# Moving columns of rounded fp32 matmuls read in pairs from both halves, PSUM written in the same order

## The chip, the cores and the metric

The kernel runs on one core of one Trainium2 chip. The metric is the device time of one execution in microseconds; the median of several runs is compared. A core has five engines that run their own queues and wait for each other by semaphores: PE (matrix products; the profile shows its weight loads apart, as PEld), DVE (vector work), ACT (functions and copies), POOL (general vector work, and a DMA queue) and SP (issues most DMAs). Matmuls write PSUM, eight banks of 512 fp32 columns on each of 128 partitions; only DVE and ACT read it here. Everything else works on SBUF.

## The reference

A layer norm feeds two branches, full attention with 32 heads of 18 features over 2048 tokens, and a gated feed-forward block of 4608 hidden features. Their product is added to the input:

```python
def reference(A_x, A_wqkv, A_wo, B_x, B_W_gate, B_W_up, B_W_down):
    # S = 2048 tokens, D = 576, H = 32 heads, F = 4608
    ...
        p = _softmax(scores, axis=-1)
        o = jnp.einsum("bhqk,bhkd->bhqd", p, v)
    ...
        gate = gate * (lambda x, dt: x.astype(dt))(gate > 0, gate.dtype)
        h = gate * up
        return jnp.einsum("bsf,fd->bsd", h, W_down)

    xn = _layernorm(x, axis=-1)
    s = _A_ref(xn, A_wqkv, A_wo)
    g = _silu(_B_ref(xn, B_W_gate, B_W_up, B_W_down))
    return x + s * g
```

All inputs and the output are fp32.

## The kernel before

**Products in three parts.** Most fp32 operands are split into two rounded numbers of the type float32r: `hi`, the value rounded, and `lo`, what is left. A product is then three matmuls of rounded operands (`PRODUCTS`: hi by hi, hi by lo, lo by hi), all added up in one PSUM bank. Only the product of the softmax terms with the values (tile `po`) is of plain fp32.

**A matmul's two operands.** `nc.tensor.matmul(ps, l, r)` loads `l`, the stationary operand (up to 128 columns), into the array and streams `r`, the moving operand, through it, column by column: 512 columns in most products here, 288 (half of D) in the others. For each moving column one column of `ps` is written or added to. All matmuls of the kernel go through the helper `mm` (line 274), so they all have the profile's line L275; the tiles tell them apart.

**Two lanes.** A matmul over 64 rows uses half of the array's rows. The kernel keeps two such streams going, lane 0 on partitions 0 to 63 and lane 1 on 64 to 127, each writing a bank of its own at any time. The class `Lanes` writes out PE's order by hand: it keeps a clock for each lane, charges a matmul `cols * COL + FIX` us (COL 0.000446, FIX 0.006), and picks the next matmul, the bank and the engine that empties it from these estimates. A sum of many matmuls (`Part`) begins in one lane and is ended in the other. `keep` holds the instructions in the order in which they are recorded.

**The stages.** First the tokens are normalized and transposed (`tps`), in four groups of 512. Their products with the attention weights give queries and keys (`pq`, 512 columns) and values (`pv`, 288 columns). From then on the feed-forward block and the attention share PE, in cycles: `pg` and `pu` are the gate and up products (512 columns), `py` the down product (288 columns), `pm` and `psx` are the two passes over the attention scores (512 columns; the first for the row maxima, the second for the exponentials), `po` the product with the values. DVE reduces `pm` to maxima (L401), ACT turns `psx` into exponentials (L891), DVE and ACT empty the others, and POOL splits the weights (L312, L313) and the hidden features (L744, L747). At the end the attention's output weights are applied (`pw`, 288 columns, all 128 rows at once, one matmul after the other).

**The warm-up.** `busy` (line 607) keeps PE at work while the first loads arrive: 8 matmuls on a tile of ones, then 24 on `xr`, a rounded copy of the first tokens. Its results are not used. The 24 differ, four by four, in the order in which the moving columns are read (`mixed`), and the last four have 32 stationary columns in place of 128. PSUM is written in order in all of them.

Of the kernel before, what the change touches and what calls it, by code (L numbers as in the profile page):

```python
# [10 lines left out]
F32R = mybir.dt.float32r  # L11
# [206 lines left out]
def kernel(  # L218
# [10 lines left out]
    nc = tc.nc  # L229
    P = 128  # L230
# [34 lines left out]
    def keep(ins):  # L265
        return tc.keep_in_program_order(ins)
# [4 lines left out]
        ins = nc.sync.dma_start(*args)  # L271
        return keep(ins) if in_order[0] else ins

    def mm(*args, **kw):
        return keep(nc.tensor.matmul(*args, **kw))  # L275

    def tp(*args):
        return keep(nc.tensor.transpose(*args))
# [14 lines left out]
    def bank(b, name):  # L293
        return banks.tile([P, 512], F32, tag=f"b{b}", name=name)

    def fence(by, ps):
        eng = {"A": nc.scalar, "V": nc.vector}[by]
        eng.clobber_nop(outs=[eng.lower_ap(ps)])

    lanes = Lanes(8, bank, mm, fence)  # L300

    def lane_rows(lane):
# [128 lines left out]
    with ExitStack() as st:  # L431
# [175 lines left out]
        def busy(xt):  # L607

            ones = one.tile([P, 512], F32R, name="ones")
            xr = one.tile([P, 576], F32R, name="xr")  # L610
            root = one.tile([P, 1], F32, name="root")
            nc.gpsimd.memset(ones.bitcast(F32), 1.0)
            nc.scalar.activation(root, ident[:, :1], AF.Sqrt)
            nc.scalar.activation(xr, xt[:, 0], AF.Copy)
            ps = bank(7, "wu")
            def mixed(form, **n):
                return xr[:, :512].rearrange(f"p {form}", **n)

            ops = [(ones[:, :P], ones)] * 8 + [(xr[:, :P], xr[:, :512])] * 4
            ops += [(xr[:, :P], mixed("(a b) -> p b a", b=2))] * 4  # L620
            ops += [(xr[:, :P], mixed("(a b) -> p b a", a=2))] * 4
            ops += [(xr[:, :P], mixed("(a b) -> p b a", b=16))] * 4
            ops += [(xr[:, :P], mixed("(a b c) -> p b a c", a=32, c=4))] * 4
            ops += [(xr[:, :32], xr[:, :512])] * 4
            for l, r in ops:
                m = l.shape[1]
                to = ps[:m]
                if len(r.shape) == 3:
                    to = to.rearrange("p (a b) -> p a b", b=r.shape[2])
                if len(r.shape) == 4:  # L630
                    to = to.rearrange("p (a b c) -> p a b c", b=r.shape[2], c=r.shape[3])
                mm(to, l, r, start=True, stop=True)
            nc.scalar.activation(root, ps[:, :1], AF.Copy)

        ln0 = []
        xt0 = load_rows(0)
        busy(xt0)
        for _ in stats(xt0, ln0):
            pass
# [267 lines left out]
    def attend(u, qp):  # L907

        va = vas[u % 2]
        b, ps = lanes.hold("po")  # L910
        batch = sorted(ready, key=lambda r: r[0])
        for n, (kt, p) in enumerate(batch):
            for i in range(2):
                for h in range(2):
                    s_ = 32 * (2 * h + i)
                    mm(
                        ps[s_ : s_ + 32, :], va[:, kt, h * VA : h * VA + 32], p[:, h, i, :],
                        start=(n == 0), stop=(n == len(batch) - 1), skip_group_check=True,
                    )
        end = lanes.pause(len(batch) * 0.86 + 0.3)  # L920
        ready.clear()

        def copy(ps):
            ots.append(two.tile([P, 512], F32, name="ot", bufs=2))
            nc.scalar.activation(ots[0], ps, AF.Copy)

        def add(ps):
            ot = ots.pop()
            keep(nc.vector.tensor_tensor(ot, ps, ot, ALU.add))  # L929
            later.append(divide(u, qp, ot))  # L930

        lanes.evict(b, ps, end, [("V", 0.69, add)] if ots else [("A", 0.6, copy)])
# [35 lines left out]
    for k in range(0, N1, 2):  # L968
# [6 lines left out]
        n = 7 if i % 2 == 0 else 6  # L975
# [83 lines left out]
    def any_bank(name):  # L1059
        turns[0] += 1  # L1060
        return bank(turns[0] % 8, name)
# [27 lines left out]
    for j in range(4):  # L1089
        js = slice(j * P, (j + 1) * P)  # L1090
        for n in range(2):
            cs = halves[n]
            ps = any_bank("py")[:, :HC]
# [8 lines left out]
    for i, k in enumerate(horder):  # L1102
# [8 lines left out]
        for cs in halves:  # L1111
            ps = any_bank("pw")[:, :HC]
# [39 lines left out]
```

## Time and profile before

| what | value |
|---|---|
| median of 3 runs | 2610.64 us (2610.39 to 2611.22) |
| the profiled execution | 2609.53 us, its span 2607.8 us |
| PE busy | 2575.4 us, 25308 matmuls |
| DVE, ACT, POOL busy | 1785.9, 1471.0, 1440.5 us |
| moved by DMA | 241.85 MB, mean 93 GB/s |

The span is the time from the first to the last instruction that the profiler saw. A matmul's row gives its start and its duration; durations of matmuls that follow each other overlap, because they are pipelined, so the pace is read from one start to the next. In a name such as `64*128 64x512` the first part is the stationary operand (rows by columns), the second the moving one.

### The profile page before, as it was taken

What the parts mean: (1) busy time and instruction counts of PE and PEld (TensorE: products, weight loads), DVE (VectorE), ACT (ScalarE), POOL (GpSimd) and SP (SyncE); (2) the same over time, 40 slices, a digit from 0 to 9 for tenths busy, and PEclk for the clock granted to TensorE, in tenths of its full rate; (3) what the DMA queues carried; (4) which work ended last, traced back from release to release, by engine and by line L of the source; (5) the groups of instructions that cost most, each with busy time, mean ns of one, the idle gap of its engine ahead of it and who ended that gap; (6) DMA issues with size and microseconds to landing.
All of it is one profiled execution on the core that took longest, in us unless ns stands there. A gap on an engine that the chain in (4) does not pass through costs nothing.

```text
span 2607.8 us, 62736 instructions
## 1 busy us (share of the span) xinstructions
PE 2575.4 (99%) x25308; PEld 2106.7 (81%) x25308; DVE 1785.9 (68%) x2976; ACT 1471.0 (56%) x2763; POOL 1440.5 (55%) x1276
## 2 busy tenths in 40 slices
PE   8999999999999999999999999999999999999998
PEld 6998887777778887777778778788878777777778
DVE  4326557777777777777777777777777777776137
ACT  3221136666666666666666666666666666666662
POOL 4236885555555555555555555555555555555554
PEclk8999999999999999999999999999999999999999
DMA  7645332222332222222242222222232222222237
GB/s 240 219 150 150 88 103 69 78 70 72 98 100 66 76 69 75 69 70 75 74 133 72 71 72 67 74 66 77 72 114 82 66 77 72 74 67 58 58 113 214
DMA packets 270353, 241.85 MB, mean 93 GB/s; under 512 B 33904, under 2 KB 214896, under 8 KB 270064
## 3 DMA queue, kind: packets, MB, share of 16 engines
q1 hardware_dynamic: 262000, 209.53, 27.5%
q0 software_dynamic: 8064, 28.32, 3.3%
q8 instruction: 200, 3.28, 0.5%
q14 instruction: 89, 0.73, 0.1%
HBM read 192.79 MB, written 44.96 MB: 91 GB/s over the span
## 4 chain that ended last, share of the span: by engine, by line
PE 92%; DMA 3%; POOL 2%; DVE 1%; SPq 1%; issue 1%; ACT 0%; POOLq 0%; DVEq 0%; ACTq 0%
PE pg L275 19%; PE po L275 17%; PE py L275 16%; PE pu L275 15%; PE pm L275 10%; PE psx L275 9%; PE pq L275 3%; PE pv L275 2%; SPq L271 1%; PE pw L275 1%; DMA rgw<-in_A_wqkv_dram 0%; DMA qd<-hh 0%; DMA gt<-yd 0%; DMA rg<-in_B_W_up_dram 0%; DMA kT<-kd 0%
## 5 line engine op out<-in xcount | busy, mean ns | idle before, releaser
L401 DVE TENSOR_REDUCE mx<-pm 128x1 f32<-128x512 f32 x2048 | 1378.5, 689 | 351.5 <-PE pm L275 207.1
L891 ACT ACTIVATE p<-psx 128x512 f32<-128x512 f32 x2048 | 1181.9, 598 | 567.4 <-PE pm L275 279.3
L275 PE MATMUL pg<-x,gw 64*128 64x512 f32 x3888 | 1155.2, 391 | 1.8 <-POOL gw L313 1.8
L275 PE MATMUL pu<-x,gw 64*128 64x512 f32 x3888 | 1141.7, 391 | 0.0
L275 PE MATMUL pm<-kT,qT 54*128 54x512 f32 x2048 | 792.2, 397 | 0.7 <-DMA kT<-kd 0.7
L275 PE MATMUL psx<-qT,kT 56*128 56x512 f32 x2048 | 786.7, 394 | 0.0
L275 PEld LDWEIGHTS pg<-x,gw 64*128 64x128 f32 x3888 | 718.5, 186 | 43.4 <-POOL gw L313 2.7
L275 PEld LDWEIGHTS pu<-x,gw 64*128 64x128 f32 x3888 | 716.2, 186 | 33.5
L275 PE MATMUL py<-dw,hh 64*128 64x288 f32 x6864 | 720.3, 295 | 5.7 <-DVE ot L929 3.1
L275 PEld LDWEIGHTS py<-dw,hh 64*128 64x128 f32 x6864 | 665.4, 186 | 74.2 <-issue 53.4
L275 PE MATMUL po<-p,va 128*32 128x512 f32 x4096 | 452.7, 594 | 0.4 <-ACT p L891 0.4
L744 POOL CAST hh<-h 128x512 fp32r<-128x512 f32 x127 | 77.6, 611 | 607.2 <-DVE h L741 607.2
L313 POOL TENSOR_TENSOR gw<-rg,gw 128x1152 fp32r<-128x1152 f32 x144 | 383.7, 2665 | 11.6
L275 PEld LDWEIGHTS psx<-qT,kT 56*128 56x128 f32 x2048 | 375.3, 185 | 17.8
L275 PEld LDWEIGHTS pm<-kT,qT 54*128 54x128 f32 x2048 | 371.6, 185 | 15.6 <-DVE mx L401 0.9
L771 POOL TENSOR_TENSOR y<-yt,y 128x288 f32<-128x288 f32 x268 | 215.0, 806 | 297.8 <-ACT yt L770 297.6
L275 PEld LDWEIGHTS po<-p,va 128*32 128x32 f32 x4096 | 126.4, 110 | 279.1 <-issue 269.1
L313 POOL TENSOR_TENSOR dw<-rd,dw 128x576 fp32r<-128x576 f32 x144 | 212.2, 1474 | 11.5
L747 POOL TENSOR_TENSOR hh<-h,hh 128x512 fp32r<-128x512 f32 x144 | 186.2, 1293 | 33.2 <-ACT hh L746 23.1
L312 POOL CAST gw<-rg 128x1152 fp32r<-128x1152 f32 x144 | 165.0, 1146 | 23.4 <-DMA rg<-in_B_W_up_dram 9.5
L766 DVE TENSOR_TENSOR y<-py,y 128x288 f32<-128x288 f32 x268 | 120.0, 448 | 58.7 <-PE py L275 58.5
L929 DVE TENSOR_TENSOR ot<-po,ot 128x512 f32<-128x512 f32 x32 | 22.1, 691 | 188.4 <-PE po L275 188.4
(92 smaller groups left out, 1421.2 us busy)
## 6 DMA issues: line engine op xcount, KB each, us to landing
rd<-in_B_W_down_dram SPq DMA_DIRECT2D x144, 288.0 KB
rg<-in_B_W_gate_dram SPq DMA_DIRECT2D x144, 256.0 KB
rg<-in_B_W_up_dram SPq DMA_DIRECT2D x144, 256.0 KB
qT<-qd SPq DMA_DIRECT2D x384, 36.0 KB
kT<-kd SPq DMA_DIRECT2D x384, 36.0 KB
kd<-hh POOLq DMA_DIRECT2D x16, 512.0 KB, 5.5
qd<-hh POOLq DMA_DIRECT2D x16, 512.0 KB, 6.1
xTd<-x SPq DMA_DIRECT2D x15, 512.0 KB
```

What stands on the lines that cost most here:

```text
L271: ins = nc.sync.dma_start(*args)
L275: return keep(nc.tensor.matmul(*args, **kw))
L312: keep(nc.gpsimd.tensor_copy(hi, raw))
L313: keep(nc.gpsimd.tensor_tensor(lo, raw, hi.bitcast(F32), ALU.subtract))
L401: keep(nc.vector.tensor_reduce(mx[:, g % 2, h, j, c : c + 1], ps, axis=AX.X, op=ALU.max))
L744: keep(nc.gpsimd.tensor_copy(hh[:, 0], h))
L747: keep(nc.gpsimd.tensor_tensor(hh[:, 1], h, hh[:, 0].bitcast(F32), ALU.subtract))
L766: keep(nc.vector.tensor_tensor(ys[j][:, cs], ps[:, :HC], ys[j][:, cs], ALU.add))
L771: keep(nc.gpsimd.tensor_tensor(ys[j][:, cs], t, ys[j][:, cs], ALU.add))
L891: nc.scalar.activation(p[0][:, h, i, :], ps, AF.Exp, scale=SCALE)
L929: keep(nc.vector.tensor_tensor(ot, ps, ot, ALU.add))
```

## The change

`mm` now looks at the moving operand. If that is float32r and a plain two-dimensional view, both it and the PSUM view are given another order of columns by `paired`: with n columns, the order is 0, 1, n/2, n/2+1, 2, 3, n/2+2, n/2+3 and so on. Each moving column still ends in the PSUM column of its own number, so nothing else has to know of it. The stationary operand, the plain fp32 products (`po`) and the transposes (`tp`) stay as they are. The planner's constants in `Lanes` stay too.

The warm-up gets another list: 18 matmuls on ones in order, then three each of six orders, with `ones` as the stationary operand. In five of them PSUM is written in the order of the reading, in the last one in sequence (`both` is 0). Views with more than two dimensions pass through `mm` unchanged. `mm` moves from line 275 to line 281.

```diff
-    def mm(*args, **kw):
-        return keep(nc.tensor.matmul(*args, **kw))
+    def paired(t):
+        return t.rearrange("p (a b c) -> p b a c", a=2, c=2)
+
+    def mm(ps, l, r, **kw):
+
+        if r.dtype == F32R and len(r.shape) == 2:
+            ps, r = paired(ps), paired(r)
+        return keep(nc.tensor.matmul(ps, l, r, **kw))
...
             ps = bank(7, "wu")
-            def mixed(form, **n):
-                return xr[:, :512].rearrange(f"p {form}", **n)
-
-            ops = [(ones[:, :P], ones)] * 8 + [(xr[:, :P], xr[:, :512])] * 4
-            ops += [(xr[:, :P], mixed("(a b) -> p b a", b=2))] * 4
-            ops += [(xr[:, :P], mixed("(a b) -> p b a", a=2))] * 4
-            ops += [(xr[:, :P], mixed("(a b) -> p b a", b=16))] * 4
-            ops += [(xr[:, :P], mixed("(a b c) -> p b a c", a=32, c=4))] * 4
-            ops += [(xr[:, :32], xr[:, :512])] * 4
-            for l, r in ops:
...
+            ops = [(ones, 512, 1, 512, 1)] * 18
+            ops += [(xr, 512, 2, 2, 1)] * 3 + [(xr, 512, 2, 4, 1)] * 3 + [(xr, 512, 4, 2, 1)] * 3
+            ops += [(xr, 512, 2, 8, 1)] * 3 + [(xr, 288, 2, 2, 1)] * 3 + [(xr, 288, 2, 1, 0)] * 3
+            for r, n, a, c, both in ops:
+                r, to = (t[:, :n].rearrange("p (a b c) -> p b a c", a=a, c=c) for t in (r, ps))
+                if not both:
+                    to = ps[:, :n].rearrange("p (b a c) -> p b a c", a=a, c=c)
+                mm(to, ones[:, :P], r, start=True, stop=True)
```

More of the change, by code (lines that the diff above doesn't have):

```diff
@@ L615, in busy @@
             ps = bank(7, "wu")
-            def mixed(form, **n):
-                return xr[:, :512].rearrange(f"p {form}", **n)
-            ops = [(ones[:, :P], ones)] * 8 + [(xr[:, :P], xr[:, :512])] * 4
-            ops += [(xr[:, :P], mixed("(a b) -> p b a", b=2))] * 4
-            ops += [(xr[:, :P], mixed("(a b) -> p b a", a=2))] * 4
-            ops += [(xr[:, :P], mixed("(a b) -> p b a", b=16))] * 4
-            ops += [(xr[:, :P], mixed("(a b c) -> p b a c", a=32, c=4))] * 4
-            ops += [(xr[:, :32], xr[:, :512])] * 4
-            for l, r in ops:
[L626 to L632, printed above, removed]
+            ops = [(ones, 512, 1, 512, 1)] * 18
[6 more added lines that the diff above has]
+                mm(to, ones[:, :P], r, start=True, stop=True)
             nc.scalar.activation(root, ps[:, :1], AF.Copy)
```

## The prediction

> **What bounds the kernel now.** I read the page's shares first, then the chain of waits, then PE's groups by form, then single matmuls on the timeline.
>
> ```profile
> span 2607.8 us, 62736 instructions
> PE 2575.4 (99%) x25308; PEld 2106.7 (81%) x25308; DVE 1785.9 (68%) x2976; ACT 1471.0 (56%) x2763; POOL 1440.5 (55%) x1276
> PE 92%; DMA 3%; POOL 2%; DVE 1%; SPq 1%; issue 1%; ACT 0%; POOLq 0%; DVEq 0%; ACTq 0%
> ```
>
> PE is never idle for more than 32.4 us in all, and 92% of the chain that ended last is PE behind itself. So the end is set by how fast matmuls follow each other, and that is what the change touches. Busy share alone does not tell the pace, since matmuls overlap. The pace comes from start times; the counts come from the groups (line, engine, tiles, stationary and moving shape, count | busy us, mean ns | idle before):
>
> ```profile
> L275 PE MATMUL pg<-x,gw 64*128 64x512 f32 x3888 | 1155.2, 391 | 1.8 <-POOL gw L313 1.8
> L275 PE MATMUL pu<-x,gw 64*128 64x512 f32 x3888 | 1141.7, 391 | 0.0
> L275 PE MATMUL pm<-kT,qT 54*128 54x512 f32 x2048 | 792.2, 397 | 0.7 <-DMA kT<-kd 0.7
> L275 PE MATMUL psx<-qT,kT 56*128 56x512 f32 x2048 | 786.7, 394 | 0.0
> L275 PE MATMUL py<-dw,hh 64*128 64x288 f32 x6816 | 712.2, 295 | 2.7 <-POOL dw L313 1.5 <-ACTq L298 0.2
> L275 PE MATMUL po<-p,va 128*32 128x512 f32 x4096 | 452.7, 594 | 0.4 <-ACT p L891 0.4
> L275 PE MATMUL pq<-x,wqk 64*128 64x512 f32 x972 | 124.0, 398 | 0.7 <-ACT x L519 0.7
> L275 PE MATMUL pv<-wv,x 64*128 64x288 f32 x864 | 65.4, 299 | 9.0 <-DVEq L298 9.0
> L275 PE MATMUL pw<-wo,hf 128*128 128x288 f32 x384 | 56.3, 295 | 0.5 <-DVE hf L1067 0.5
> ```
>
> All but po have rounded fp32 on the moving side, so all but po are changed. Two-lane matmuls of 512 columns: 3888 + 3888 + 2048 + 2048 + 972 = 12844, two at a time, so 6422 slots. Two-lane matmuls of 288: 6816 + 864 = 7680, so 3840 slots. About 496 of 288 columns use all 128 rows and run alone (384 here, 64 more of pw, 48 of py at the end).
>
> The slots, on the timeline (start us, us, engine, line):
>
> ```profile
> 1500.71 0.39 PE L275 MATMUL pu<-x,gw 64*128 64x512 f32 x1
> 1500.94 0.39 PE L275 MATMUL pu<-x,gw 64*128 64x512 f32 x1
> ...
> 1503.04 0.40 PE L275 MATMUL pu<-x,gw 64*128 64x512 f32 x1
> 1503.21 0.29 PE L275 MATMUL py<-dw,hh 64*128 64x288 f32 x1
> ...
> 1503.34 0.29 PE L275 MATMUL py<-dw,hh 64*128 64x288 f32 x1
> 1503.47 0.39 PE L275 MATMUL pm<-kT,qT 54*128 54x512 f32 x1
> 2575.71 1.76 PE L275 MATMUL pw<-wo,hf 128*128 128x288 f32 x12
> ```
>
> In one lane a 512-column matmul starts every (1503.04 - 1500.71) / 10 = 0.233 us. A 288-column one lasts to the next start 0.13 us. The lone pw run gives the third digit: (1.76 - 0.29) / 11 = 0.134 us. So a slot costs 0.0025 to 0.006 us plus about 0.445 ns a column. The sum of slots: 6422 x 0.2335 = 1500, 3840 x 0.134 = 515, 496 x 0.134 = 66, and po 453: 2534 us of the 2607.8. The rest is idle time, warm-up, transposes and lanes alone.
>
> **What reading order does to the pace.** The warm-up in busy() already holds matmuls of 512 columns that differ only in the order of their moving columns. By the code's order they are, four each: contiguous; every second column; a column of the first half and one of the second by turns; every sixteenth column; runs of four, 64 bytes apart; contiguous with 32 stationary columns.
>
> ```profile
> PEclk8999999999999999999999999999999999999999
> 5.04 1.91 PE L275 MATMUL wu<-xr 128*128 128x512 f32 x4
> 7.20 1.53 PE L275 MATMUL wu<-xr 128*128 128x512 f32 x3
> 8.11 0.63 PE L275 MATMUL wu<-xr 128*128 128x512 f32 x1
> 8.79 0.81 PE L275 MATMUL wu<-xr 128*128 128x512 f32 x3
> 9.22 0.38 PE L275 MATMUL wu<-xr 128*128 128x512 f32 x1
> 9.86 1.48 PE L275 MATMUL wu<-xr 128*128 128x512 f32 x3
> 10.72 0.61 PE L275 MATMUL wu<-xr 128*128 128x512 f32 x1
> 11.40 0.83 PE L275 MATMUL wu<-xr 128*128 128x512 f32 x3
> 11.84 0.39 PE L275 MATMUL wu<-xr 128*128 128x512 f32 x1
> 12.30 0.85 PE L275 MATMUL wu<-xr 128*32 128x512 f32 x3
> 12.77 0.39 PE L275 MATMUL wu<-xr 128*32 128x512 f32 x1
> ```
>
> Each row of three with the row of its last gives two steps: every second column (8.11 - 7.20) / 2 = 0.455; halves by turns 0.215; every sixteenth 0.43; runs of four 0.22; contiguous with 32 columns 0.235. The first row, (1.91 - 0.63) / 3 = 0.427, is contiguous at what I take for a reduced clock: the page's clock row is below 9 in its first slice, and the later contiguous rows are near 0.233. So at the clock of the main loops contiguous reading costs 0.233, here and in the loops, while halves by turns cost 0.215, 8% less. Order of reading alone moves the pace, both ways.
>
> The new order is 0, 1, 256, 257, 2, 3, ...: by turns between the halves like the 0.215 row, with two neighbours each time like a contiguous read. I expect no less than the 0.215 row's pace from the read. The Trainium skill, Advanced Engine Details and Errata, section SBUF Cachelines, says that two accesses to the same 16-byte line are needed for full pace. This trace disagrees: halves by turns never hit a line twice in a row and are the fastest row; by that rule the new order would be as good as the old, and the sum would be nothing.
>
> **The change part by part.** *Instructions.* The order of all engines stays; only PE's warm-up is another list, and a few waits of PE on PE are new. PE's start, before (wu is the warm-up's bank, ones and xr its operands):
>
> ```order
> L275 MATMUL wu<-ones 128x512 x8
> L275 MATMUL wu<-xr 128x512 x20
> L275 MATMUL wu<-xr 32x512 x4
> L278 MATMUL tps<-ident,xn 128x64 x24
> L275 MATMUL pq<-x,wqk_167 128x512 x13
> ```
>
> and now:
>
> ```order
> L281 MATMUL wu<-ones 128x512 x18
> L281 MATMUL wu<-xr,ones 128x128x2x2 x3
> L281 MATMUL wu<-xr,ones 128x64x2x4 x3
> L281 MATMUL wu<-xr,ones 128x64x4x2 x3
> L281 MATMUL wu<-xr,ones 128x32x2x8 x3
> L281 MATMUL wu<-xr,ones 128x72x2x2 x3
> L281 MATMUL wu<-xr,ones 128x288 x3
> L284 MATMUL tps<-ident,xn 128x64 x24
> L281 MATMUL pq<-x,wqk_171 128x128x2x2 x13
> ```
>
> The transposes and pq stand where they stood. Warm-up, 32 before, 36 now: some 14 at 0.427, 4 at 0.233, 12 at 0.215 and 6 at 0.124 make 10.2 us against 11.6; at 0.43 for the odd ones 13 or 14. I count 0, with 2 us either way.
>
> *New waits.* PE rows that wait on PE's own semaphore rise from 15 to 156. A typical place is after a batch of po (p are softmax terms, va values), before:
>
> ```order
> L275 MATMUL po<-p,va_3011 32x512 [waits Activation_49]
> L275 MATMUL po<-p,va_3011 32x512
> L275 MATMUL py<-dw,hh 128x288 [waits DVE_49,Pool_49]
> L275 MATMUL py<-dw,hh 128x288 x3
> L275 MATMUL py<-dw,hh 128x288 [waits Pool_49]
> ```
>
> and now:
>
> ```order
> L281 MATMUL po<-p,va_3015 32x512 [waits Activation_49]
> L281 MATMUL po<-p,va_3015 32x512
> L281 MATMUL py<-dw,hh 128x72x2x2 [waits DVE_49,Pool_49]
> L281 MATMUL py<-dw,hh 128x72x2x2 [waits PE_49]
> L281 MATMUL py<-dw,hh 128x72x2x2 x2
> L281 MATMUL py<-dw,hh 128x72x2x2 [waits Pool_49]
> ```
>
> The second py, the other lane's first, now waits for a matmul that stands ahead of the whole po batch, done microseconds earlier. All of PE queues behind it, but there is nothing left to wait for: 0, at most 141 x 0.134 = 19 us if each lost a slot.
>
> *The read.* 512 columns: lower bound 0.215, upper bound inside a gain 0.2225 (runs of four). I take 0.217, next to the row it resembles most. Gain 6422 x (0.2335 - 0.217) = 106 us. 288 columns have no row; scaled, 0.121 (0.215 x 288 / 512) to 0.128. I take 0.1245: 3840 x 0.0095 = 36 us, and 496 x 0.0095 = 5 us. Sum 147 us. po keeps its 453.
>
> *The write.* No matmul of this trace writes PSUM out of order. The nearest rows are the reads: between 0.215 (halves by turns) and 0.455 (every second column) for 512. I take no cost, because pairs stay neighbours and the warm-up's jumps over half a tile were free on the read side. The other end is a rival below. The Trainium skill speaks on both sides: PSUM — Partial Sum Buffer, section Specifications (TRN2), says that any non-contiguous pattern slows matmuls significantly, and Advanced Engine Details and Errata, section PSUM Cachelines, asks only that every two consecutive elements be contiguous, which this order keeps. No run here shows either.
>
> *What could take the gain back.* Issue and weight loads must follow a 0.062 us step in py:
>
> ```profile
> 13.09 0.97 PE L278 MATMUL tps<-ident,xn 64*128 64x64 f32 x24
> L275 PEld LDWEIGHTS py<-dw,hh 64*128 64x128 f32 x6816 | 657.5, 186 | 70.2 <-issue 49.5 <-POOL dw L313 3.3 <-ACTq L298 2.4
> L275 PEld LDWEIGHTS po<-p,va 128*32 128x32 f32 x4096 | 126.4, 110 | 279.1 <-issue 269.1 <-ACT p L891 10.0
> 0.00:60.00 60.00, 48.90 (x388) 38.18 (x388) 29.40 (x69) 19.72 (x42) 30.17 (x28) 0.93 0.73 226
> 270.00:330.00 60.00, 57.44 (x594) 50.92 (x592) 31.80 (x56) 10.07 (x22) 50.46 (x48) 1.00 0.33 97
> 500.00:1000.00 500.00, 500.00 (x4917) 396.65 (x4915) 376.46 (x615) 312.25 (x580) 273.82 (x239) 1.00 0.27 80
> ```
>
> 24 transposes with their loads went out in 0.97 us, 0.040 each, so issue is not the limit. A load of 128 columns lasts 186 ns, of 32 columns 110: 0.79 ns a column, estimated 0.101 us of a lane's 0.1245. That is close, and cuts py's gain if I am 0.02 off. In the windows (length, then busy us of PE, PEld, DVE, ACT, POOL; granted clock; DMA share and GB/s) DVE fills 75% of the steady stretch and would fill 80%, ACT and POOL less. At 270 to 330 us POOL is at 84% with PE at 96%, and in the first 60 us PE is busy for 48.9 only, with the transfers at 0.73; there some of the gain is lost. I take off 12 us, 6% of 200 us of such stretches.
>
> Net 147 - 12 = 135. The profiled execution took 2609.53 us (span 2607.8, 1.7 around it): 2474.5, and the median of the runs is 1.1 above it: **2475 us**. Its own range: all at 0.215 and 0.121, nothing lost, gain 6422 x 0.0185 + 4336 x 0.013 = 175, so 2435; at 0.2225 and 0.128 with 20 lost, 71 + 26 - 20 = 77, so 2530.
>
> **The rivals.** *The write sets the pace.* If each step to another place in PSUM costs as a read of every sixteenth or second column does, a 512 slot takes 0.43 to 0.455 and a 288 slot 0.242 to 0.256. Added: 6422 x 0.1965 + 4336 x 0.108 = 1730 us to 6422 x 0.2215 + 4336 x 0.122 = 1951: about 4340 to 4560 us. It decides as soon as a paired slot costs over 0.2335. For it: an access of another place each time doubled two warm-up rows. Against: two others lost nothing. The rule of the Trainium skill's page PSUM — Partial Sum Buffer, named above, would end here.
>
> *Only 288 columns are slow.* Their halves lie 576 bytes apart, not 1024, and no row shows that distance. At 0.256 they cost 4336 x 0.122 = 529 us more and 512 gains its 106: about 3030. Smaller mixtures of either kind end between 2616 and 3000.
>
> *Nothing changes.* If 0.233 is the price of two lanes' loads and not of the order, the time stays at 2610. Against it: the lone-lane contiguous rows have the same 0.235 and 0.134. Half of the gain (288 unmoved, new waits at their bound) would be 2520 to 2600.
>
> **How the numbers follow.** Both sides follow the fast row 0.55, a smaller gain 0.07, within 0.2% (what a measurement of this kernel can tell from no change) 0.06, slower up to 3030 us 0.13, the write at about double 0.19. Faster 0.62, same 0.06, slower 0.32. The range runs from 2435 to 3050: 0.81 less a little at its low end. Forecast alone: 2435 to 2530.
>
> **What would show it.** Right: in the new trace pg and pu of one lane start 0.215 to 0.22 us apart, py 0.122 to 0.127; po stays at 453 us busy; the warm-up rows of shape 128x2x2 step by 0.215 and DVE's share rises to 72%. Wrong on the write: the 128x2x2 warm-up rows, which read and write in that order, step above 0.233. Wrong on 288: py alone above 0.134. If pg steps at 0.217 and the time hardly falls, waits on DVE, POOL or loads stand in PE's idle time.

## The result, and the profile after

The changed kernel takes 3425.22 us (median of 4 runs, 3424.29 to 3427.13) against 2610.93 us for the kernel before (4 runs): 1.312 times as long, with an interval of 1.3097 to 1.3143. The forecast was 2475 us, so even the direction was wrong, and the time lies beyond the upper end of the range, 3050 us. No rival had this time either: it lies between the 3030 us of slow 288-column products and the 4340 us of a slow write.

The page of the changed kernel begins so (span; busy us and share by engine; the chain that ended last, by engine):

```profile
span 3425.4 us, 62804 instructions
PE 3410.8 (100%) x25312; PEld 2665.8 (78%) x25312; DVE 1831.4 (53%) x2976; ACT 1522.0 (44%) x2763; POOL 1428.6 (42%) x1276
PE 97%; DMA 1%; issue 1%; SPq 1%; POOL 1%; DVE 0%; POOLq 0%; ACT 0%; DVEq 0%; ACTq 0%
```

Idle time of PE falls from 32.4 to 14.6 us (3425.4 - 3410.8). No new wait holds PE up; it is PE itself that takes longer. The groups by form (busy us, mean ns of one) say which matmuls:

```profile
L281 PE MATMUL pg<-x,gw 64*128 64x512 f32 x3888 | 1554.2, 503 | 0.0
L281 PE MATMUL pu<-x,gw 64*128 64x512 f32 x3888 | 1541.3, 501 | 0.0
L281 PE MATMUL pm<-kT,qT 54*128 54x512 f32 x2048 | 1011.1, 504 | 0.0
L281 PE MATMUL psx<-qT,kT 56*128 56x512 f32 x2048 | 1001.5, 503 | 0.0
L281 PE MATMUL py<-dw,hh 64*128 64x288 f32 x6816 | 954.4, 361 | 0.0
L281 PE MATMUL po<-p,va 128*32 128x512 f32 x4096 | 452.7, 594 | 0.0
```

Every kind whose columns were reordered grew: pg from 391 to 503 ns, py from 295 to 361. po, which keeps its order, has the same 452.7 us to the tenth. The timeline gives the step from start to start in one lane, and the last row a run of lone matmuls of 288 columns:

```profile
1500.33 0.51 PE L281 MATMUL pg<-x,gw 64*128 64x512 f32 x1
...
1500.66 0.50 PE L281 MATMUL pg<-x,gw 64*128 64x512 f32 x1
...
1503.30 0.50 PE L281 MATMUL pg<-x,gw 64*128 64x512 f32 x1
...
3369.68 2.04 PE L281 MATMUL pw<-wo,hf 128*128 128x288 f32 x10
```

From 1500.33 to 1503.30 that lane has nine steps, 0.330 us each, where it was 0.233. The pw run steps by (2.04 - 0.36) / 9 = 0.187 us, where it was 0.134. With the prediction's counts, 6422 x (0.330 - 0.2335) + 4336 x (0.187 - 0.134) = 620 + 230 = 850 us. The time grew by 814. Of the 36 us between, 18 are PE's idle time that fell; where the other 18 went was not traced. So the whole loss stands in the slots, and the question is which side of the reordering makes them longer. The changed kernel's own warm-up can't tell: its three matmuls that read and write in the new order start 0.33 us apart (the first at 7.35, the third at 8.01 us). That is the sign by which the prediction would have called the write wrong, but these matmuls reorder both sides, as the loops do.

### The profile page after: what moved, and what is told of

Same layout as the page of the kernel before. It is cut to its first block, busy times and chain, and to the rows that moved or that the text cites. A ratio compares the mean times of both kernels' runs of the same rounds, so it can differ in the third digit from the quotient of the medians.

```text
span 3425.4 us, 62804 instructions
## 1 busy us (share of the span) xinstructions
PE 3410.8 (100%) x25312; PEld 2665.8 (78%) x25312; DVE 1831.4 (53%) x2976; ACT 1522.0 (44%) x2763; POOL 1428.6 (42%) x1276
## 4 chain that ended last, share of the span: by engine, by line
PE 97%; DMA 1%; issue 1%; SPq 1%; POOL 1%; DVE 0%; POOLq 0%; ACT 0%; DVEq 0%; ACTq 0%
PE pg L281 24%; PE py L281 18%; PE pu L281 14%; PE po L281 13%; PE psx L281 11%; PE pm L281 10%; PE pq L281 4%; PE pv L281 2%; PE pw L281 1%; DMA rgw<-in_A_wqkv_dram 1%; SPq L271 0%; DMA qd<-hh 0%; POOL wqk L319 0%; DMA o<-od 0%; PE tps L284 0%
## 5 line engine op out<-in xcount | busy, mean ns | idle before, releaser
L888 ACT ACTIVATE p<-psx 128x512 f32<-128x512 f32 x2048 | 1208.9, 598 | 1117.6 <-PE psx L281 746.1
L281 PE MATMUL pg<-x,gw 64*128 64x512 f32 x3888 | 1554.2, 503 | 0.0
L281 PE MATMUL pu<-x,gw 64*128 64x512 f32 x3888 | 1541.3, 501 | 0.0
L281 PE MATMUL pm<-kT,qT 54*128 54x512 f32 x2048 | 1011.1, 504 | 0.0
L281 PE MATMUL psx<-qT,kT 56*128 56x512 f32 x2048 | 1001.5, 503 | 0.0
L281 PE MATMUL py<-dw,hh 64*128 64x288 f32 x6864 | 964.4, 361 | 3.6 <-DVE ot L926 3.6
L281 PEld LDWEIGHTS py<-dw,hh 64*128 64x128 f32 x6864 | 861.0, 193 | 101.8 <-issue 55.6
L281 PEld LDWEIGHTS pg<-x,gw 64*128 64x128 f32 x3888 | 754.0, 194 | 160.2
L281 PEld LDWEIGHTS pu<-x,gw 64*128 64x128 f32 x3888 | 753.2, 194 | 66.5
L281 PE MATMUL po<-p,va 128*32 128x512 f32 x4096 | 452.7, 594 | 0.0
L281 PE MATMUL pq<-x,wqk 64*128 64x512 f32 x972 | 171.0, 501 | 0.3 <-ACT x L525 0.2
```

Of the source, the lines that this page charges most:

```text
L281: return keep(nc.tensor.matmul(ps, l, r, **kw))
L888: nc.scalar.activation(p[0][:, h, i, :], ps, AF.Exp, scale=SCALE)
```

## The experiments

| kernel | median us | ratio to the kernel before (95% interval) |
|---|---|---|
| pairs read, straight write | 3424.14 | 1.3121 (1.3102 to 1.3141) |
| straight read, pairs written | 2609.56 | 1.0007 (0.9990 to 1.0023) |
| orders apart, in the warm-up alone | 2612.97, one run | only its warm-up is read |
| line hits, in the warm-up alone | 2614.72, one run | only its warm-up is read |
| halves by turns, put in order on the exit | 2485.92 | 0.9526 (0.9511 to 0.9540) |
| the same, planner refitted | 2519.22 | 0.9649 (0.9633 to 0.9665) |

The kernel before was timed again beside them: 2609.85 us (median of 13 runs), and 2610.38 us (7 runs) beside the refitted planner.

### The read alone

```diff
+    def in_turn_order(t):
+        return t.rearrange("p (b a c) -> p b a c", a=2, c=2)
...
-            ps, r = paired(ps), paired(r)
+            ps, r = in_turn_order(ps), paired(r)
```

> The moving columns are read in the new order, PSUM is written straight through; the columns of every changed product land in another order, so the output is not the reference's. Theory W (the PSUM write in pairs is what costs): the slot of 512 columns falls to about 0.217 us and the time to about 2475 us. Theory R (the read in pairs from two halves is what costs): slot 0.328 us, time about 3425 us, as in the changed kernel. Theory B (each side costs a part): slot between 0.235 and 0.32 us, time between 2620 and 3380 us.

Measured: 3424.14 us, all of the loss. The timeline of this kernel, one lane:

```profile
1500.55 0.50 PE L284 MATMUL pu<-x,gw 64*128 64x512 f32 x1
...
1500.88 0.50 PE L284 MATMUL pm<-kT,qT 54*128 54x512 f32 x1
...
1502.86 0.50 PE L284 MATMUL pu<-x,gw 64*128 64x512 f32 x1
```

Seven steps in 2.31 us, 0.330 each. Theory W, which is the prediction's main rival and blames PSUM, would have had 0.217 here. It falls.

### The write alone

```diff
-            ps, r = paired(ps), paired(r)
+            ps, r = paired(ps), in_turn_order(r)
```

> The moving columns are read straight through, PSUM is written in pairs from both halves (output columns in another order, so not the reference's). Theory W: slot 0.328 us, about 3425 us. Theory R: slot 0.2335 us, about 2610 us. Theory B: between 2620 and 3380 us, and the two extras of this kernel and of the one with the read alone add up to about 815 us.

Measured: 2609.56 us, the same as before. The timeline of this kernel, one lane:

```profile
1499.95 0.40 PE L284 MATMUL pg<-x,gw 64*128 64x512 f32 x1
...
1500.19 0.39 PE L284 MATMUL pg<-x,gw 64*128 64x512 f32 x1
...
1500.65 0.39 PE L284 MATMUL pg<-x,gw 64*128 64x512 f32 x1
```

Three steps in 0.70 us: 0.233, the old slot. Writing PSUM in pairs from both halves costs nothing that can be measured, and there is nothing for theory B to share out. This kernel has as many of the added waits of PE on PE as the changed one, so they are cleared of the loss too.

### Orders apart, in the warm-up

The loops of the kernel before, with another list in busy(): `rd` and `wr` say whether the moving view and the PSUM view get the new order.

```diff
+            ops += [(xr, 512, 2, 2, 1, 0)] * 4 + [(xr, 512, 2, 2, 0, 1)] * 4 + [(xr, 512, 2, 2, 1, 1)] * 4
+            ops += [(xr, 512, 2, 1, 1, 0)] * 4
...
+            ops += [(xr, 288, 2, 2, 1, 0)] * 4 + [(xr, 288, 2, 2, 0, 1)] * 4
+            ops += [(xr, 288, 2, 1, 1, 0)] * 4 + [(xr, 512, 2, 2, 0, 0)] * 4
+            for r, n, a, c, rd, wr in ops:
+                r = (view if rd else straight)(r, n, a, c)
+                to = (view if wr else straight)(ps, n, a, c)
+                mm(to, ones[:, :P], r, start=True, stop=True)
```

> The loops of the kernel before; only the warm-up differs: four matmuls of each kind, read order and write order apart. Theory W: 512 columns with pairs read and a straight write step by 0.215 to 0.22 us, straight read with pairs written by 0.333 us or more, both by 0.335 us; 288 columns 0.123 and 0.186 us. Theory R: pairs read and a straight write step by 0.335 us (288: 0.186), straight read with pairs written by 0.233 us (288: 0.132). Both theories: one column of each half by turns with a straight write 0.215 us (288: 0.123). The time is within 10 us of 2611 us.

On this kernel's timeline each kind gives a row with its last three matmuls and one with the last alone; half the difference of their starts is the step. In order: pairs read; pairs written; halves by turns read; runs of four read by turns from the halves; then of 288 columns pairs read, halves by turns read:

```profile
7.42 1.19 PE L275 MATMUL wu<-xr,ones 128*128 128x512 f32 x3
8.09 0.51 PE L275 MATMUL wu<-xr,ones 128*128 128x512 f32 x1
8.68 0.86 PE L275 MATMUL wu<-xr,ones 128*128 128x512 f32 x3
9.14 0.40 PE L275 MATMUL wu<-xr,ones 128*128 128x512 f32 x1
...
10.93 0.81 PE L275 MATMUL wu<-xr,ones 128*128 128x512 f32 x3
11.36 0.38 PE L275 MATMUL wu<-xr,ones 128*128 128x512 f32 x1
11.82 0.92 PE L275 MATMUL wu<-xr,ones 128*128 128x512 f32 x3
12.32 0.42 PE L275 MATMUL wu<-xr,ones 128*128 128x512 f32 x1
...
15.69 0.73 PE L275 MATMUL wu<-xr,ones 128*128 128x288 f32 x3
16.07 0.36 PE L275 MATMUL wu<-xr,ones 128*128 128x288 f32 x1
...
16.92 0.53 PE L275 MATMUL wu<-xr,ones 128*128 128x288 f32 x3
17.16 0.29 PE L275 MATMUL wu<-xr,ones 128*128 128x288 f32 x1
```

The steps are 0.335, 0.23, 0.215, 0.25, then 0.19 and 0.12 us. Of the rows left out here, pairs on both sides step by 0.335 like pairs read alone, runs of four and of eight written alone by 0.23, quarters read singly by 0.27, and 288 columns with pairs written by 0.135. Theory R on every row that it priced; it had no price for the runs of four. The order that the prediction took for a sibling of the fast row is half as slow again as that row, alone in the warm-up, with one lane and without accumulation. So the loss needs neither the two lanes nor the loops.

### What a read order must keep together

The two orders differ only in that one takes columns of the halves singly and the other in pairs. Thirteen orders on a larger tile of ones tell three theories on that apart. In the list the first pair of numbers is the outermost (step in columns, count):

```diff
+            for dims in (
+                ((1, 256), (1024, 2)),
+                ((4, 128), (1, 2), (1024, 2)),
+                ((4, 256), (1024, 2)),
+                ((2, 128), (1024, 2), (1, 2)),
+                ((4, 256), (1, 2)),
+                ((8, 128), (1, 4)),
+                ((16, 64), (1, 8)),
+                ((1, 256), (1, 2)),
+                ((1, 256), (4, 2)),
+                ((1, 256), (8, 2)),
+                ((1, 256), (16, 2)),
+                ((1, 128), (512, 4)),
+                ((1, 512),),
+            ):
+                reads += [dims] * 4
```

> The loops of the kernel before; only the warm-up differs: four matmuls of 512 columns each, on a tile of ones, straight PSUM write, thirteen read orders. Theory P (even and odd columns are fetched by two paths, and each path needs several successive columns of its own in one 16-byte line): halves by turns 0.215 us; halves by turns with two columns of each line 0.22 to 0.25; with one column of each line above 0.27; pairs by turns 0.33; two neighbours of each line, lines in sequence, above 0.3; columns i and i+d by turns 0.215 for d of 1, 4, 8 and 16. Theory L (two successive columns in one line are enough, jumps cost otherwise): two neighbours of each line 0.22 to 0.235, halves by turns with one column of each line above 0.3. Theory D (only the distance between successive columns counts): halves by turns 0.215 however many columns of a line are used, columns i and i+1 0.233. Time within 10 us of 2611.

Four of the thirteen, as pairs of rows like those above: two columns of each line, halves by turns; one column of each line, halves by turns; two neighbours of each line; columns i and i+1:

```profile
11.37 0.85 PE L275 MATMUL wu<-src,ones 128*128 128x512 f32 x3
11.82 0.40 PE L275 MATMUL wu<-src,ones 128*128 128x512 f32 x1
12.49 1.54 PE L275 MATMUL wu<-src,ones 128*128 128x512 f32 x3
13.40 0.64 PE L275 MATMUL wu<-src,ones 128*128 128x512 f32 x1
...
15.62 1.54 PE L275 MATMUL wu<-src,ones 128*128 128x512 f32 x3
16.52 0.64 PE L275 MATMUL wu<-src,ones 128*128 128x512 f32 x1
...
19.07 0.81 PE L275 MATMUL wu<-src,ones 128*128 128x512 f32 x3
19.50 0.38 PE L275 MATMUL wu<-src,ones 128*128 128x512 f32 x1
```

All thirteen, worked out in the same way from the start times, and one order of the warm-up above. A line here is the 16 bytes, four columns, of the section on lines that the prediction cites; the middle column counts how many of a line's columns come in succession among the even places of the order (the odd places give the same):

| order of the columns | of a line, in succession, among every second place | step, us |
|---|---|---|
| halves by turns | 4 | 0.215 |
| i and i+1, i+4, i+8, i+16 by turns | 4 | 0.215 each |
| straight | 2 | 0.23 |
| halves by turns, two of each line | 2 | 0.23 |
| runs of four, every other line | 2 | 0.235 |
| runs of eight, every other pair of lines | 2 | 0.23 |
| runs of four from the halves by turns (warm-up above) | 2 | 0.25 |
| quarters by turns | 1, two lines alternate | 0.27 |
| pairs of the halves by turns (the change) | 1, two lines alternate | 0.325 |
| halves by turns, one of each line | 1, a new line each time | 0.455 |
| two neighbours of each line | 1, a new line each time | 0.45 |

Theory P fits every order that it priced, though the 0.33 of the pairs was known when it was written. For the quarters it had no price, and the runs of four are at the slow end of what it allows for two of a line. Theory D falls with i and i+1, which lie next to each other and are as fast as columns 1024 apart, and with the halves by turns that use one column of each line. Theory L falls with the two neighbours of each line: they stay on a line for two successive columns, and the step is 0.45, twice the 0.22 to 0.235 that it asked for. That even and odd columns take two paths is inferred from these times; no record of the trace shows a path. Why two alternating lines cost less than a new line each time, why quarters are cheaper than pairs, and why runs of four by turns cost more than straight reading is open.

### The order that was meant, on the exit side

Halves by turns, one column each, keeps four. PSUM is then written straight, and whatever empties a bank reads every second PSUM column to put the order right; the maxima need no order.

```diff
-            ps, r = paired(ps), paired(r)
+            ps, r = straight(ps), by_turns(r)
...
-            nc.scalar.activation(made[0], ps, AF.Relu)
+            nc.scalar.activation(halves_(made[0]), sorted_(ps), AF.Relu)
...
-            keep(nc.vector.tensor_tensor(h, ps, h, ALU.mult))
+            keep(nc.vector.tensor_tensor(halves_(h), sorted_(ps), halves_(h), ALU.mult))
```

(`by_turns` is "p (a b) -> p b a", `straight` "p (b a) -> p b a", `sorted_` "p (b a) -> p a b" and `halves_` "p (a b) -> p a b", with a = 2. The other readers of the changed products are edited in the same way.)

> One column of each half by turns on the read side, PSUM written straight through, and the order put right by the instruction that empties the bank (it reads every second PSUM column; the maxima need no order). Nothing is left out. Under either theory the slot falls to 0.2155 us for 512 and 0.1225 us for 288 columns, and the time to 2460 to 2490 us, if DVE and ACT read every second PSUM column as fast as they read straight (0.69 and 0.60 us for 512). If such reads take twice as long, ACT's exponentials alone grow by 1200 us to 2670 us busy and the time is above 2700 us.

Measured: 2485.92 us, 4.7% less than the kernel before. Its page begins as the first block shows; the second has the two ends of a stretch of one lane on its timeline, and a run of lone matmuls of 288 columns:

```profile
span 2486.1 us, 62852 instructions
PE 2442.7 (98%) x25312; PEld 1986.2 (80%) x25312; DVE 1758.5 (71%) x2976; ACT 1459.9 (59%) x2763; POOL 1429.1 (57%) x1276
```

```profile
1500.98 0.38 PE L290 MATMUL pg<-x,gw 64*128 64x512 f32 x1
...
1501.86 0.37 PE L290 MATMUL pg<-x,gw 64*128 64x512 f32 x1
...
2450.98 1.63 PE L290 MATMUL pw<-wo,hf 128*128 128x288 f32 x12
```

Four steps of that lane in 0.88 us, 0.22 each; ten steps that end in the same row, from 1499.68 us on, give 0.218. The lone pw run steps by (1.63 - 0.29) / 11 = 0.122 us. The readers of PSUM, DVE's product and ACT's exponentials in this kernel:

```profile
L748 DVE TENSOR_TENSOR h<-pu,h 128x512 f32<-128x512 f32 x144 | 99.0, 687 | 52.4 <-ACT h L744 31.2 <-PE pu L290 14.6 <-PE py L290 6.4
L898 ACT ACTIVATE p<-psx 128x512 f32<-128x512 f32 x2048 | 1175.8, 597 | 481.2 <-PE pm L290 252.3 <-PE psx L290 179.8 <-PE pg L290 9.6
```

687 and 597 ns, against 689 and 598 in the kernel before: for both of these, reading every second fp32 of PSUM is free. PE's idle time is 43.4 us (2486.1 - 2442.7) against 32.4 before.

### The planner refitted

```diff
-    COL, FIX, EVICT, SERVE, FENCE = 0.000446, 0.006, 0.28, 0.08, 0.15
+    COL, FIX, EVICT, SERVE, FENCE = 0.000415, 0.004, 0.28, 0.08, 0.15
```

> The kernel with halves read by turns and the order put right on the exit, with the planner's COL and FIX set to the new slots (0.000415 and 0.004 in place of 0.000446 and 0.006), so that lanes, banks and fences are planned for the pace that PE has. If the 30 us or so by which 2486 us stand above the slot sum are banks and fences planned too late, 2465 to 2480 us; if the plan hardly matters, 2480 to 2490 us.

Measured: 2519.22 us, a miss of both: 33 us slower than with the old constants. Its page has

```profile
PE 2475.6 (98%) x25312; PEld 2047.4 (81%) x25312; DVE 1806.2 (72%) x2976; ACT 1465.9 (58%) x2763; POOL 1428.8 (57%) x1276
```

in a span of 2518.0 us: PE's idle time is 42.4, no more than with the old constants, and its busy time is 32.9 us longer for the same matmuls. That may be stretches with one lane alone; it was not followed up. The constants that are nearer to the slots make the slower order here, and why is open.

## Why the prediction was wrong

**What bounds the kernel** was right. PE's slots set the time; the loss of 814 us and the gain of 124 us (2610 to 2486) both came through them.

**The read** is the step that failed: "I expect no less than the 0.215 row's pace from the read." The slot became 0.330 us, not 0.217. The new order was called a blend of two rows, the by-turns one and the straight one, and priced by the first. But here the mixture of two orders was slower than either. By the count that the later runs bear out, the warm-up rows of the kernel before read so: every second column is a new line at every second place (0.455), every sixteenth too (0.43), straight and runs of four have two of a line there (0.233 and 0.22), halves by turns four (0.215). The new order has one, with two lines that alternate, and came out between, at 0.330. No row of the kernel before had that order, so its price could not be read there. But a bound for the read out to the slow rows, 0.43 to 0.455, was owed; the range inside the read ended at 0.2225, and slow rows were used for the write alone.

**The first warm-up row** was read with a wrong reason. The prediction took its 0.427 for a reduced clock, by the low first digit of the page's clock row. But the granted clock in the trace is 1.00 from 5.0 to 6.7 us; what lowers that digit is 0.60 from 34 to 38 us and 0.56 from 54 to 65 us. That the row is slow for another reason than its order does hold: in the warm-up with the orders apart, straight matmuls on ones step by 0.427 us up to 3.76 and by 0.228 from 4.58 us on. What makes the first ones slow is not shown, and no other row is read by it.

**The line rule** was set aside too soon. The Trainium skill, Advanced Engine Details and Errata, section SBUF Cachelines, asks for two accesses to a 16-byte line. The runs agree if the accesses are counted for even and odd places apart: with two or more the step is 0.215 to 0.25, with one 0.27 to 0.455. Counted for successive columns, as the prediction read it, they disagree, in the by-turns row (0.215) and in the two neighbours of each line (0.45).

**The write** was priced at nothing, and that was right: 2609.56 us with the write alone. Its rival, given 0.19, blamed the wrong side of the same edit. The Trainium skill has two sentences on PSUM. By the one, any pattern that is not contiguous slows matmuls significantly (PSUM — Partial Sum Buffer, section Specifications (TRN2)); this run (1.0007 times the time before, slot 0.233) disagrees, in pairs at least. The other asks that every two consecutive elements be contiguous (Advanced Engine Details and Errata, section PSUM Cachelines); the same numbers agree with that. That section has the first sentence too, so the prediction's "asks only" is not right. No run here writes single columns out of order.

**288 columns only** fell: 512 columns slowed by a factor of 1.41 (0.330 / 0.2335), 288 by 1.40 (0.187 / 0.134); halves 576 and 1024 bytes apart are slowed alike.

**The new waits of PE on PE** cost nothing that shows, as priced: the kernel with the write alone has them and keeps the time, and PE's idle time fell in the changed kernel.

**The sum** nearly holds for another order, halves by turns with the exit put right: slots of 0.218 to 0.22 and 0.122 us, and 2486 us where 2475 was forecast for slots of 0.217 and 0.1245. By these slots and the prediction's counts some 139 to 152 us should be saved (6422 x 0.0135 to 0.0155, and 4336 x 0.012), and 124 were. So the losses are some 15 to 28 us where 12 were taken off; PE's idle time, 11 us longer, is part of them. Issue and weight loads did follow: 24 matmuls of py in two lanes, from 318.85 us on, take 1.63 us, so twelve slots of two follow each other in (1.63 - 0.28) / 11 = 0.12 us. One end of the prediction's range is off by its own terms: 2611 less 77 is 2534, not 2530.

## What to carry to other kernels

When a kernel is bound by matmul slots, the order in which the moving columns are read is worth measuring: for these rounded fp32 operands straight reading costs 0.233 us per 512 columns, and two streams of neighbouring columns by turns 0.215. A row is evidence for its own order only; before a neighbour of it goes into 20000 matmuls, four matmuls of exactly that order in the warm-up settle the price. And where an edit reorders a read and a write together, run each alone: here one cost everything and the other nothing.

## What the runs showed of the hardware

- A straight read of rounded fp32 columns is not the fastest: 0.227 to 0.235 us per 512 against 0.215 for two streams of neighbouring columns by turns, at distances of 1, 4, 8, 16, 256 and 1024 columns.
- Two streams from the two halves take 0.325 to 0.335 us in pairs by turns, and 0.25 in runs of four.
- PSUM written in pairs out of order, and PSUM read by DVE and ACT at every second fp32, keep full pace (slot 0.233; 687 and 597 ns for 512).
- The plain fp32 product po kept its 452.7 us beside all this; its reads, in straight order, were not touched.
